# A new hand-written order for the first twelve blocks of an attention kernel, with P of blocks 0 to 3 transposed per token tile and 13 idle products instead of 22

## The chip, the core and the metric

The kernel runs on one core of one Trainium2 chip. The metric is the device time of one launch in microseconds (us). Three runs of the kernel before gave 808.72 us as their median (808.2 to 810.61). A difference under about 0.3% (2.4 us) cannot be told from no change.

## What is computed

The input `x` has 2048 tokens of 640 values and is layer-normalised to `xn`. Branch A is attention of 32 heads with 192 values per head, over the last 512 keys of a cache; branch B gives two selected tokens an extra feed-forward term and serves as a gate.

```
xn = layernorm(A_x)
q  = (xn @ wq) in 32 heads of 192
p  = softmax(q @ k_window^T * 192**-0.5)        # 512 keys
s  = concat(p @ v_window) @ wo
r  = xn @ w_r;  idx = the two tokens with the largest r
b  = xn, with sigmoid(r) * ffn(xn) added at idx
out = x + s * silu(b)
```

## The kernel before, in words

**Tiles and blocks.** The 32 heads are 8 groups of 4 heads, and a group is two pairs. The tokens are four stretches `t5` of 512, each of four token tiles of 128. A *step* is one group, one stretch and one pair of heads (`steps`); a *block* is half a step, that is two token tiles (a = 0, 1) of one pair of heads. There are 64 steps and 128 blocks, and blocks 0 and 1 belong to step 0, blocks 2 and 3 to step 1, and so on.

**The work of block b.** Q is the product of `xnT` with `wq` for a step, in three column parts c (`q_whole` in the head, L309, evicted to `qT` by ScalarE at L315 or VectorE at L313; from block 12 on, and for steps 5 to 7 in the head, in two phases `qa` and `qb` by `q_phase`, L340, evicted at L350 and L352). `S.b.a` is the scores of token tile a against the pair's keys (`scores`, L367), into one of two PSUM buffers `ps_s`. `M.b.a` is the negative row maximum on VectorE (L372). `E.b.a` is two exponentials on ScalarE (L377), one for each head, into `p_ring`; they also free the scores' buffer. P is then transposed by a DMA transpose on SyncE's queue into `pT_ring`: once for both token tiles after `E.b.1` (L383), or, for blocks listed in `SPLIT`, once after each `E.b.a` (L381). `P.b` is the product of pT with V (`o_item`, L406), whose result is scaled by the reciprocal of the row sums (L413) into `o_sb`: with "va" one head on VectorE (L417) and the other on ScalarE (L420), with "vv" both on VectorE, with "av" the two changed about. A DMA transpose makes `oT` (L423). `W.k` is the product of oT with `wo` (`w_item`, L447), added into `s_acc` by VectorE (L468) or, with "a", ScalarE (L466).

**The order.** The schedule is written by hand (`manual_schedule`): each engine runs its instructions in the order in which the Python code emits them. Blocks 0 to 11 (`HEAD = 12`) follow the list of tokens in `FIRST`, each passed to `first(token)`. From block 12 on all blocks follow the same list `BLOCK`, in which P lags by two blocks and W by six, and the last two follow `LAST`. The head also holds the layer norm: loads of x (`x.t5.part` and the loads ahead of the list), statistics (`bn`, `st` on VectorE, `sa` on ScalarE for three tiles of stretch 3), the reciprocal deviation (`dev`, `nw`), the normalisation of a token tile (`app`, `ap` on VectorE "v", ScalarE "a" or GpSimd "g"), and its transposition to `xnT` by TensorE and a copy (`turn`, L282 and L283), or for stretch 3 by one DMA transpose (`xT`, L515). `kturn` transposes the first pair's keys on TensorE (L276, copies at L277); for other pairs GpSimd reorders the keys (`ko`, L121) and a DMA transposes them (`kT`, L125). `v`, `k`, `wq`, `wo` are loads of their tensors on SyncE's queue; `wd` copies half of wo on GpSimd (L151). `exp` loads ScalarE's table for the exponential (L543). `B.b` emits the loads and other items that are due at block b.

**Queues.** All loads and DMA transposes of the list stand in SyncE's queue, in the order of their tokens; a transpose that waits for its data holds up what is behind it. Each DMA also waits for the DMA that last used its semaphore, and there are eight of these.

**Idle products.** Ahead of all this TensorE runs 22 products of a tile of zeros with itself (L163), whose result nobody reads, while the first loads and statistics are under way.

The block list that every block from 12 on follows, and the rule for the transposes of P:

```
    BLOCK = "A S0 M0 W m E0 B S1 M1 P E1 l".split()
...
        if b in SPLIT:
            nc.sync.dma_start_transpose(out=pT_ring[:, b % RP, a], ...
        elif a == 1 and b < NB - 1:
            nc.sync.dma_start_transpose(out=pT_ring[:, b % RP].rearrange(...
```

Of the kernel before, what the change touches and what calls it, by code (L numbers as in the profile page):

```python
# [21 lines left out]
def kernel(ctx, tc, A_x, A_k_cache, A_v_cache, A_wq, A_wo, B_x, B_w_r, B_w_gate, B_w_up, B_w_down, out):  # L22
    nc = tc.nc
    P = 128
    _, S, D = A_x.shape
# [3 lines left out]
    W = min(4096, max(256, Sk // 4))  # L29
# [44 lines left out]
    def f_tile(shape, dtype, name, kind="q"):  # L74
        return banks[kind].tile(shape, dtype, name=name, tag="f")
# [83 lines left out]
    idle = late.enter_context(tc.tile_pool(name="idle", bufs=1)).tile([P, W], BF16, name="idle")  # L159
    nc.vector.memset(idle, 0.0)  # L160
    warm_ps = f_tile([P, W], FP32, "warm_ps")
    for _ in range(22):
        nc.tensor.matmul(warm_ps, lhsT=idle[:, 0:P], rhs=idle, start=True, stop=True)  # L163

    ident_f = const.tile([P, P], FP32, name="ident_f")
# [121 lines left out]
    NS = len(steps)  # L287
    NB = 2 * NS
    HEAD = 12
    SPLIT = (NB - 4, NB - 3, NB - 2)  # L290
    qT_of = {}
    fin_x = {}
    fin_pool = {}
# [81 lines left out]
    def exps(b, a):  # L375
        for hh in range(2):
            nc.scalar.activation(out=p_ring[:, b % 2, a, :, hh, :].rearrange("p (x j) e -> p x j e", x=2),  # L377
                                 in_=s_of[b, a][:, hh, :].rearrange("p (j e x) -> p x j e", j=NJ, x=2),
                                 func=ACT.Exp, bias=nm_of[b, a][:, hh:hh + 1], scale=1.0)
        if b in SPLIT:  # L380
            nc.sync.dma_start_transpose(out=pT_ring[:, b % RP, a], in_=p_ring[:, b % 2, a].rearrange("p k h e -> p (k h e)"))  # L381
# [220 lines left out]

    def group_loads(g, b0, k0, k1, o0, t0, o1, t1, q0, q1, v0, v1, o):
# [20 lines left out]
    M = {}  # L624
# [232 lines left out]
    for fb, km in enumerate((41, 49, 57)):  # L857
# [4 lines left out]
        mul, turn = m_ffn(fb)  # L862
# [130 lines left out]
```

## Time and profile before

| | us |
|---|---|
| median of three runs | 808.72 |
| the profiled execution | 807.77 |
| its span, first to last instruction | 806.0 |
| TensorE busy | 783.0 (97%) |
| VectorE busy | 591.0 (73%) |
| ScalarE busy | 529.3 (66%) |
| GpSimd busy | 310.1 (38%) |

The profile is of one execution. Times in its views are microseconds from the start of the span. PE is TensorE's products, PEld its weight loads, DVE VectorE, ACT ScalarE, POOL GpSimd, and SPq the queue of DMA issues on SyncE; L367 is line 367 of the kernel before. Block 12, with which the fixed list begins, starts on TensorE at 90.61, so the part of the program that the change edits is the first 11% of the span. An instruction in a timeline lasts until its result is out, so that neighbours on one engine overlap a little; the chain of waits shows the distance at which they follow each other.

### The profile page before, as it was taken

The numbers are of one execution on the slowest core, as the hardware profiler recorded it, in microseconds if no ns is written. First come the engines' busy times: TensorE is split into PE (matmuls) and PEld (weight loads), VectorE is DVE, ScalarE is ACT, GpSimd is POOL, SyncE is SP. The second block draws the span as 40 slices with busy tenths as digits, with TensorE's granted clock in tenths as the row PEclk, the third lists the DMA queues.
The fourth block names the chain that finished last, engine by engine and source line by source line (L and its number), as shares of the span: only waits on it lengthen the run. The fifth ranks groups of instructions, "written<-read, shape, count | busy, mean of one in ns | idle before, by whom it ended". The sixth has DMA issues, their size and how long they took to land.

```text
span 806.0 us, 26621 instructions
## 1 busy us (share of the span) xinstructions
PE 783.0 (97%) x11354; PEld 579.1 (72%) x11354; DVE 591.0 (73%) x1086; ACT 529.3 (66%) x964; POOL 310.1 (38%) x244
## 2 busy tenths in 40 slices
PE   8799899999999999999999999999999999999997
PEld 4366577777777777777777777777777777777775
DVE  7686588778778667777666667777777777767775
ACT  5677566665666666666666667677776776666662
POOL 1312120011110100101011699959997412564865
PEclk9999999999999999999999999999999999999999
DMA  7998998798999999999998999989898899999992
GB/s 193 188 175 161 199 169 154 152 189 143 191 199 160 181 208 200 196 188 191 200 211 159 171 192 166 182 137 184 173 186 149 153 190 163 209 190 163 178 181 84
DMA packets 445111, 142.29 MB, mean 177 GB/s; under 512 B 412228, under 2 KB 444488, under 8 KB 444992
## 3 DMA queue, kind: packets, MB, share of 16 engines
q1 hardware_dynamic: 435216, 131.18, 93.1%
q10 hardware_dynamic: 8816, 6.88, 3.3%
q0 software_dynamic: 960, 2.52, 1.0%
q8 instruction: 89, 1.46, 0.8%
q14 instruction: 30, 0.25, 0.1%
HBM read 39.98 MB, written 2.62 MB: 53 GB/s over the span
## 4 chain that ended last, share of the span: by engine, by line
PE 85%; DVE 5%; DMA 4%; ACT 3%; issue 2%; POOL 0%; SPq 0%; ACTq 0%; DVEq 0%; POOLq 0%
PE w L447 24%; PE q_ps L340 21%; PE o_ps L406 18%; PE s L367 18%; DVE nm L372 2%; DMA pT<-pexp 2%; PE q_ps L309 2%; ACT o_sb L420 1%; ACT pexp L377 1%; PE warm_ps L163 1%; DMA xnT<-xn 1%; DMA oT<-o_sb 1%; DMA wo_g<-in_A_wo_dram 1%; DMA v_sb<-in_A_v_cache_dram 0%; ACT qT L315 0%
## 5 line engine op out<-in xcount | busy, mean ns | idle before, releaser
L372 DVE TENSOR_REDUCE nm<-s 128x2 f32<-128x1024 f32 x256 | 313.0, 1223 | 135.6 <-PE s L367 131.0
L377 ACT ACTIVATE pexp<-s,nm 128x512 bf16<-128x512 f32 x512 | 323.3, 688 | 90.3 <-DVE nm L372 53.9
L447 PE MATMUL w<-wo_g,oT 64*128 64x320 bf16 x3072 | 231.1, 296 | 4.8 <-ACT o_sb L420 4.5
L340 PE MATMUL q_ps<-xnT,wq_g 64*128 64x512 bf16 (+1 forms) x2340 | 232.4, 323 | 3.2 <-DMA xnT<-xn 1.5
L447 PEld LDWEIGHTS <-oT 64*128 64x128 bf16 x3072 | 171.8, 94 | 62.9 <-issue 7.5
L367 PE MATMUL s<-kT,qT 64*128 64x512 bf16 x1536 | 211.7, 376 | 5.0 <-ACT pexp L377 3.9
L406 PEld LDWEIGHTS <-pT 64*128 64x128 bf16 x4096 | 179.1, 94 | 27.9 <-issue 2.0
L406 PE MATMUL o_ps<-v_sb,pT 64*128 64x193 bf16 x4096 | 197.2, 243 | 0.0
L420 ACT ACTIVATE o_sb<-o_ps,rl 128x192 bf16<-128x192 f32 x256 | 93.6, 417 | 145.7 <-DVE rl L413 140.6
L340 PEld LDWEIGHTS <-wq_g 64*128 64x128 bf16 x2340 | 127.4, 99 | 48.3 <-issue 2.6
L151 POOL COPY wo_g<-wo_g 64x1920 bf16<-64x1920 bf16 x32 | 59.3, 1858 | 222.3 <-DMA wo_g<-in_A_wo_dram 202.1
L367 PEld LDWEIGHTS <-qT 64*128 64x128 bf16 x1536 | 85.4, 94 | 59.8 <-issue 6.4
L470 DVE TENSOR_TENSOR s_acc<-s_acc,w 128x320 f32<-128x320 f32 x192 | 85.0, 484 | 35.4 <-PE w L447 35.4
L352 ACT ACTIVATE qT<-q_ps 128x1024 bf16<-128x1024 f32 x114 | 92.4, 810 | 7.7 <-PE q_ps L340 2.8
L121 POOL COPY k_perm<-k_raw 128x768 bf16<-128x768 bf16 x30 | 25.1, 854 | 143.3 <-DMA k_raw<-in_A_k_cache_dram 111.9
L417 DVE TENSOR_TENSOR o_sb<-o_ps,rl 128x384 bf16<-128x384 f32 x128 | 71.4, 558 | 4.6 <-DVE rl L413 0.2
L831 POOL TENSOR_SCALAR yh<-y_bc,oh 128x640 bf16<-128x640 bf16 x32 | 61.7, 1929 | 3.3 <-DMA y_bc<-y_d 1.7
L832 POOL TENSOR_TENSOR xn<-xn,yh 128x640 bf16<-128x640 bf16 x32 | 44.6, 1395 | 2.7
L413 DVE RECIPROCAL rl<-o_ps 128x2 f32<-128x2 f32 x256 | 30.0, 159 | 14.4 <-PE o_ps L406 8.2
L894 POOL TENSOR_TENSOR s_acc<-s_acc,x_fin 128x640 f32<-128x640 f32 x16 | 22.4, 1397 | 31.3 <-DMA x_fin<-in_A_x_dram 30.8
L828 POOL TENSOR_SCALAR xn<-xn 128x640 bf16<-128x640 bf16 x16 | 29.4, 1838 | 0.8
L478 POOL TENSOR_TENSOR fin_o<-fin_t,s_acc 128x640 bf16<-128x640 f32 x12 | 18.5, 1540 | 17.7 <-DVE fin_t L473 11.1
(138 smaller groups left out, 262.4 us busy)
## 6 DMA issues: line engine op xcount, KB each, us to landing
wo_g<-in_A_wo_dram SPq DMA_DIRECT2D x32, 240.0 KB, 4.3
k_raw<-in_A_k_cache_dram SPq DMA_DIRECT2D x32, 192.0 KB, 3.6
v_sb<-in_A_v_cache_dram SPq DMA_DIRECT2D x32, 192.0 KB, 4.3
wq_g<-in_A_wq_dram SPq DMA_DIRECT2D x14, 288.0 KB, 4.1
wq_g<-in_A_wq_dram SPq DMA_DIRECT2D x14, 192.0 KB, 3.7
x_fin<-in_A_x_dram SPq DMA_DIRECT2D x16, 160.0 KB, 3.6
pT<-pexp SPq DMA_TRANSPOSE x130, 4.9
oT<-o_sb SPq DMA_TRANSPOSE x126, 3.4
```

What stands on the lines that cost most here:

```text
L151: nc.gpsimd.tensor_copy(out=grp[g][("wo", pr)][half(1), cs, :], in_=grp[g][("wo", pr)][half(0), cs, :])
L340: mm = nc.tensor.matmul(q_ps[k][:, 0:n] if type(q_ps) is list else q_ps[:, k, 0:n], lhsT=wq[half(r), dc, c:2 * Dh:3], rhs=xnT[half(r), tok ...
L352: nc.scalar.activation(out=out, in_=q_ps[:, :, 0:n], func=ACT.Copy, scale=scale)
L367: nc.tensor.matmul(s_of[b, a][:, r, :], lhsT=qT_of[i][half(r), c, u * P:(u + 1) * P], rhs=grp[g][("kT", pr)][half(r), :, c, :], start=(c = ...
L372: rm = nc.vector.tensor_reduce(out=nm_of[b, a], in_=s_of[b, a], axis=AX.X, op=ALU.max, negate=True)
L377: nc.scalar.activation(out=p_ring[:, b % 2, a, :, hh, :].rearrange("p (x j) e -> p x j e", x=2), in_=s_of[b, a][:, hh, :].rearrange("p (j ...
L406: nc.tensor.matmul(o_of[b][r][:, a, 0:Dh + 1], lhsT=pT_ring[half(r), b % RP, a, k, :], rhs=v_ring[half(r), (g * PAIRS + pr) % RV, k, 0:Dh ...
L417: nc.vector.tensor_tensor(out=o_sb, in0=src, in1=rl[:, r].unsqueeze(2).unsqueeze(3).to_broadcast([P, 2, 3, HK]), op=ALU.mult)
L420: nc.scalar.activation(out=o_sb[:, a], in_=src[:, a], func=ACT.Copy, scale=rl[:, r, a:a + 1])
L447: nc.tensor.matmul(w_ps[r][:, 0:HD], lhsT=oT_ring[half(r), bs[pr] % RT, c, :], rhs=grp[g][("wo", pr)][half(r), c, cs], start=(pr == 0 and ...
L470: nc.vector.tensor_tensor(out=acc, in0=acc, in1=src, op=ALU.add)
L831: nc.gpsimd.tensor_scalar(out=yh, in0=M["y_bc"][:, j, :], scalar1=M["oh"][:, n, j:j + 1], scalar2=None, op0=ALU.mult)
```

## The change

`FIRST` is written anew: the same tokens, with few exceptions, in another order. Besides the order:

- 13 idle products instead of 22;
- `SPLIT` holds blocks 0 to 3 too, so the P of each of their token tiles is transposed by a DMA of its own, as soon as that tile's exponentials are done;
- some evictions, normalisations and scalings go to another engine: `q.0.0.0` and `q.0.2.1` from VectorE to ScalarE, all of `q.2`, `q.4.1` and `q.6.2` from ScalarE to VectorE, the copies of `turn.3` and `turn.4` from ScalarE to VectorE and those of `turn.2` and `turn.6` the other way, `ap.4` to ScalarE, `ap.5`, `ap.7`, `ap.9`, `ap.14` from VectorE to GpSimd, `ap.6` and `ap.15` from GpSimd to VectorE, `ap.13` from ScalarE to GpSimd, `W.0` from ScalarE to VectorE, `W.3` and `W.5` the other way, and P.0, P.7 and P.8 are scaled by VectorE alone;
- `wq.1`, `x.1.1`, `v.1` and `x.2` are issued further ahead of the other DMAs, and the statistics of stretch 1 follow the first row maxima.

Everything from block 12 on is unchanged in the source.

```diff
-    for _ in range(22):
+    for _ in range(13):
...
-    SPLIT = (NB - 4, NB - 3, NB - 2)
+    SPLIT = (0, 1, 2, 3, NB - 4, NB - 3, NB - 2)
...
     FIRST = """
-    bn.1.0 x.1.0 bn.0.0 bn.0.1 v.0 v.1 dev.0 bn.1.1 dev.1 app.0 turn.0.a app.1 bn.3.0 turn.1.a bn.2.0 bn.2.1 dev.2 bn.3.1 kturn.av k.1.0 k.1.1 ko.1 wq.1 x.1.1 dev.3 exp st.1.0 q.0.0.0.v app.2 q.0.1.0.a kT.1 app.3 q.0.2.0.a turn.2.v turn.3.a st.1.1
-    S.0.0 S.0.1 M.0.0 q.0.0.1.a M.0.1 q.0.1.1.a q.0.2.1.v E.0.0 q.1.0.a E.0.1 v.2 v.3
-    S.1.0 st.1.2 M.1.0 st.1.3 S.1.1 M.1.1 q.1.1.a E.1.0 st.1.4 q.1.2.a E.1.1 st.1.5 st.1.6 st.1.7 x.2 wo.0 wo.1 wo.2
-    S.2.0 M.2.0 nw.1.0 nw.1.1 S.2.1 M.2.1 nw.1.2 nw.1.3 E.2.0 nw.1.4 nw.1.5 nw.1.6 ap.6.g P.0.va E.2.1 ap.4.v ap.7.v ap.5.v wo.3 wd.0 wd.1
-    S.3.0 M.3.0 turn.4.a turn.7.v S.3.1 M.3.1 turn.5.a turn.6.v E.3.0 q.2.0.a q.2.1.a P.1.va E.3.1 x.3 wd.2 wd.3 st.2.0 st.2.1 q.2.2.a st.2.2
-    S.4.0 M.4.0 q.3.0.a S.4.1 E.4.0 M.4.1 st.2.3 q.3.1.a P.2.va E.4.1 st.2.4 st.2.5 st.2.6 st.2.7
-    S.5.0 nw.2.0 M.5.0 q.3.2.a S.5.1 nw.2.1 nw.2.2 E.5.0 M.5.1 nw.2.3 nw.2.4 nw.2.5 nw.2.6 P.3.va E.5.1 ap.10.g ap.8.v sa.3.0.0
-    S.6.0 M.6.0 E.6.0 W.0.a S.6.1 M.6.1 ap.9.v ap.11.v P.4.va E.6.1 sa.3.0.1 sa.3.2.0 st.3.6 B.6
-    S.7.0 M.7.0 turn.8.v turn.11.v W.1.v turn.9.a turn.10.v S.7.1 M.7.1 E.7.0 P.5.va q.4.0.a q.4.1.a q.4.2.a E.7.1 B.7 sa.3.1.0 sa.3.2.1 st.3.7 sa.3.1.1
-    qa.5.0.1 S.8.0 B.8 nw.3.0 M.8.0 nw.3.1 nw.3.2 W.2.v qb.5.0.1 nw.3.3 S.8.1 M.8.1 E.8.0 nw.3.4 nw.3.5 nw.3.6 P.6.va E.8.1 ap.13.a ap.15.g ap.14.v ap.12.v xT.3
-    qa.5.2 S.9.0 M.9.0 B.9 W.3.v E.9.0 qb.5.2 S.9.1 M.9.1 P.7.va E.9.1
-    S.10.0 M.10.0 W.4.v E.10.0 S.10.1 M.10.1 P.8.va B.10 E.10.1
-    qa.6.0.1 S.11.0 M.11.0 W.5.v E.11.0 qb.6.0.1 S.11.1 M.11.1 P.9.va q.6.2.a E.11.1 B.11
+    v.0 bn.1.0 x.1.0 bn.0.0 bn.0.1 dev.0 bn.1.1 app.0 dev.1 x.1.1 app.1 turn.0.a wq.1 bn.3.0 bn.3.1 turn.1.a bn.2.0 v.1 k.1.0 bn.2.1 st.1.0 dev.3 k.1.1 kturn.av q.0.0.0.a dev.2 app.2 q.0.1.0.a
+    q.0.2.0.a app.3
+    S.0.0 turn.2.a x.2 v.2 ko.1 exp kT.1 turn.3.v S.0.1 q.0.1.1.a M.0.0 E.0.0 M.0.1 st.1.1 q.0.0.1.a st.1.2 q.0.2.1.a E.0.1 q.1.0.a wo.0
+    S.1.0 st.1.3 st.1.4 q.1.1.a v.3 M.1.0 st.1.5 wo.1 S.1.1 M.1.1 E.1.0 q.1.2.a E.1.1 st.1.6
+    S.2.0 st.1.7 nw.1.0 S.2.1 nw.1.1 nw.1.2 M.2.0 nw.1.3 M.2.1 wo.2 nw.1.4 E.2.0 nw.1.5 nw.1.6 E.2.1 P.0.vv ap.7.g
+    S.3.0 ap.6.v turn.7.v ap.5.g ap.4.a M.3.0 turn.4.v wd.0 st.2.0 wd.1 turn.6.a turn.5.a E.3.0 S.3.1 P.1.av wo.3 x.3 M.3.1 q.2.0.v wd.2 E.3.1 q.2.1.v st.2.1 q.2.2.v st.2.2
+    S.4.0 st.2.3 st.2.4 S.4.1 M.4.0 P.2.va E.4.0 q.3.1.a M.4.1 E.4.1 st.2.5 st.2.6 q.3.2.a st.2.7 wd.3
+    S.5.0 nw.2.0 nw.2.1 nw.2.2 M.5.0 q.3.0.a S.5.1 nw.2.3 nw.2.4 M.5.1 nw.2.5 E.5.0 W.0.v
+    S.6.0 M.6.0 nw.2.6 E.5.1 ap.10.g ap.11.v sa.3.0.0 sa.3.2.0 B.6 ap.9.g P.3.va E.6.0 S.6.1 M.6.1 P.4.va ap.8.v W.1.v E.6.1
+    S.7.0 turn.10.v turn.11.v turn.9.a turn.8.v S.7.1 st.3.6 sa.3.0.1 sa.3.1.0 M.7.0 B.7 E.7.0 q.4.1.v st.3.7 q.4.2.a M.7.1 q.4.0.a
+    qa.5.0.1 sa.3.2.1
+    S.8.0 E.7.1 M.8.0 B.8 W.2.v sa.3.1.1 nw.3.0 nw.3.1 qb.5.0.1 nw.3.2 nw.3.3 nw.3.4 nw.3.5 nw.3.6 P.5.va S.8.1 ap.13.g E.8.0 M.8.1 P.6.av E.8.1 ap.15.v ap.14.g
+    qa.5.2
+    S.9.0 S.9.1 M.9.0 ap.12.v E.9.0 qb.5.2 xT.3 M.9.1
+    S.10.0 B.9 M.10.0 E.9.1 W.3.a S.10.1 P.7.vv E.10.0 P.8.vv M.10.1 W.4.v
+    qa.6.0.1
+    S.11.0 B.10 E.10.1 M.11.0 W.5.a qb.6.0.1 P.9.va B.11 q.6.2.v S.11.1 M.11.1 E.11.0 E.11.1
     """.split()
```

## The prediction

> **What bounds the kernel now.** I read three views in this order: the busy time of each engine by stretch, TensorE's waits in the part that is edited, and TensorE's timeline there. By stretch (columns: from:to, length, then busy us of PE, PEld, DVE, ACT and POOL, granted clock, DMA share, GB/s):
>
> ```profile
> 9.00:90.61 81.61, 70.95 (x834) 43.72 (x831) 59.33 (x126) 58.96 (x121) 18.02 (x26) 1.00 0.91 176
> 90.61:180.00 89.39, 87.11 (x1276) 65.51 (x1277) 70.97 (x128) 55.88 (x101) 14.10 (x17) 1.00 0.97 169
> 180.00:404.00 224.00, 221.62 (x3305) 166.10 (x3303) 163.70 (x321) 144.59 (x261) 24.92 (x22) 1.00 1.05 187
> ```
>
> From block 12 (90.61) on TensorE is the bound: it idles 2.28 us of 89.39 and 2.38 of 224. Nothing there hangs on a fixed time, so a head that ends earlier moves all that follows. In the head TensorE idles 81.61 - 70.95 = 10.66 us, and before 9.00 it runs idle products. TensorE's largest waits up to 90.7 (total, times, longest):
>
> ```profile
> PE s L367 <- ACT pexp L377: 3.9, 5, 1.0
> PE q_ps L340 <- DMA xnT<-xn: 1.5, 1, 1.5
> PE q_ps L309 <- DVE xnT L283: 1.4, 1, 1.4
> PE tp L282 <- DVE xn L193: 1.3, 1, 1.3
> ```
>
> So it waits mostly for latency: scores for a free buffer, Q for a normalised tile. VectorE and ScalarE are busy 59 of 81.6 us, so it is their order, not their load, that makes TensorE wait. That is what a new order can win. The landmarks on TensorE:
>
> ```profile
> 1.19 7.71 PE L163 MATMUL warm_ps<-idle 128*128 128x512 bf16 x22 [1.19 <-DVE idle L160]
> 13.27 1.47 PE L367 MATMUL s<-kT,qT 64*128 64x512 bf16 x12
> 23.26 0.88 PE L367 MATMUL s<-kT,qT 64*128 64x512 bf16 x6 [0.76 <-ACT pexp L377]
> 46.41 0.82 PE L367 MATMUL s<-kT,qT 64*128 64x512 bf16 x6 [0.34 <-ACT pexp L377]
> 82.12 1.26 PE L340 MATMUL q_ps<-xnT,wq_g 64*128 64x512 bf16 x10 [1.48 <-DMA xnT<-xn]
> 90.61 1.26 PE L340 MATMUL q_ps<-xnT,wq_g 64*128 64x512 bf16 x10 [0.69 <-ACT qT L315]
> ```
>
> These are the idle products, S.0.0 with S.0.1, S.2.0, S.5.1, the first phase of qa.6.0.1 and the start of block 12.
>
> **The idle products.** Their weight loads show the pace:
>
> ```profile
> 6.28 0.15 PEld L163 LDWEIGHTS <-idle 128*128 128x128 bf16 x1 [0.28 <-issue]
> 6.71 1.69 PEld L163 LDWEIGHTS <-idle 128*128 128x128 bf16 x8 [0.28 <-issue]
> ```
>
> ```profile
> PEclk9999999999999999999999999999999999999999
> ```
>
> Up to 6.71 one product takes 0.43 us, after that 1.69 / 8 = 0.21: TensorE's pace doubles near 7, after 5.5 us at half. The page's clock row shows nothing of it, so only the pace tells. Thirteen at 0.43 end at 1.19 + 5.55 = 6.74, not 8.9. The first work behind them needs the first normalised tile, whose statistics come in the same order on VectorE as before:
>
> ```profile
> 5.99 0.45 DVE L264 TENSOR_SCALAR xn<-x_in,mv,rstd 128x640 bf16<-128x640 bf16 x1
> 18.43 1.23 DVE L372 TENSOR_REDUCE nm<-s 128x2 f32<-128x1024 f32 x1 [1.08 <-PE s L367]
> 36.88 0.56 DVE L417 TENSOR_TENSOR o_sb<-o_ps,rl 128x384 bf16<-128x384 f32 x1
> ```
>
> Ready at 6.44, it waited 2.4 us for the products; now 0.3. So 2.1 us is won at that point, if the pace is not lost. [...] What a late switch costs I bound from the rows by themselves: a second spell at half pace as long as the first, 5.5 us from 6.74 on, loses at most half of it, so 0 to 2.8. I take 0.5, near the low end, because the work that follows starts at once and the copies between leave room.
>
> **The walk through the new order.** I walked the new list by hand, each engine in its order, with these durations. TensorE's distances, from the chain of waits:
>
> ```profile
> 112.03 1.64 PE w L447 x24
> 113.67 0.55 PE q_ps L340 x10
> 114.22 0.65 PE s L367 x6
> 114.86 1.35 PE o_ps L406 x32
> 116.21 1.08 PE q_ps L340 x10
> ```
>
> ScalarE and GpSimd:
>
> ```profile
> 9.21 1.29 ACT L283 COPY xnT<-tp 128x640 bf16<-128x640 bf16 x2 [2.95 <-PE tp L282]
> 10.58 0.80 ACT L277 COPY kT<-tp_k 128x768 bf16<-128x768 bf16 x1
> 11.59 1.28 ACT L543 ACT_TABLE_LOAD   x1
> 21.95 1.26 ACT L377 ACTIVATE pexp<-s,nm 128x512 bf16<-128x512 f32 x2
> 35.15 0.60 ACT L315 ACTIVATE qT<-q_ps 128x512 bf16<-128x512 f32 x1 [0.48 <-PE q_ps L309]
> ```
> ```profile
> 12.55 1.72 POOL L121 COPY k_perm<-k_raw 128x768 bf16<-128x768 bf16 x2 [10.76 <-DMA k_raw<-in_A_k_cache_dram]
> ```
>
> DMA transposes (issue in ns, min/median/max; landing after the issue; the first two rows are the head's whole transposes of P, the next two the tail's, mostly of one token tile):
>
> ```profile
> L383 SPq DMA_TRANSPOSE pT<-pexp x11: 1697/1992/5461, 19.4 to 88.9; - x11
> DMA to landing us min/median/max: 4.3/4.5/9.1
> ```
> ```profile
> L381 SPq DMA_TRANSPOSE pT<-pexp x6: 1232/1323/2166, 770.9 to 782.7; - x6
> DMA to landing us min/median/max: 3.1/4.8/5.2
> ```
> ```profile
> kT<-k_perm SPq DMA_TRANSPOSE x2, 3.9
> xnT<-xn SPq DMA_TRANSPOSE x1, 6.9
> ```
>
> *To S.0.0.* Transposes of tiles 0 and 1 and of the keys (about 0.3, 0.3, 0.7 at full pace) run from 6.74 to 8.3; ScalarE copies the two tiles by 8.4; three Q products of 256 columns (0.55 each, 1.65) end at 10.2; ScalarE's last eviction ends at 10.75. The statistics `st.1.0` now stand ahead of VectorE's copy of the keys and wait for x of stretch 1, so that copy ends near 10.5, just in time. S.0.0 starts at 10.8, not 13.27: 2.5 us.
>
> *To S.2.0.* S.0.1 follows only after tiles 2 and 3 (12.05), since their normalisation stands behind. The maxima end at 13.65 and 14.8; the table load (1.28, now behind the copy of tile 2) ends at 13.7; with three evictions between, E.0.0 ends at 15.2 and E.0.1 at 16.95. S.1.0 starts at 15.85, S.1.1 at 17.6, the evictions of q.1 end at 20.0, and S.2.0 starts at 20.05, not 23.26: 3.2 us. The keys of the pair must be there: loads land near 12.2, GpSimd's copies (1.72) end at 13.9, the transpose lands near 18.4. `x.2` is issued ahead of it, its 640 KB, as slow as the row below, spend that margin at worst.
>
> ```profile
> x_in<-in_A_x_dram SPq DMA_DIRECT2D x2, 640.0 KB, 6.0
> SPq L383 <- ACT pexp L377: 19.4, 8, 3.7
> ```
>
> *To S.4.0 and S.5.1.* The split counts here. P.0 starts at 21.95. E.0.1 ends at 16.95, the second half is issued at 17.0 and lands 4.8 later, at 21.8. SyncE issues 2 x 1.32 instead of 1.99 for a block, 2.6 us more over four; its queue waited 19.4 us for exponentials at L383 alone (the row above, SyncE's waits up to 100), which hides that, and if the queue fills it costs up to 2.6. Tiles 4 to 7 are normalised on three engines while P.0 and S.3.0 run, so the two waits of 1.3 and 1.4 for them shrink to one of 0.9. The evictions of q.2 go to VectorE, which ends them at 32.65 while ScalarE does E.3.1 (31.55). S.4.0 is over at 33.1 and S.5.1 starts at 39.25, not 46.41: 7.2 us.
>
> *To block 12.* W.0 is late next: its oT of block 2 is issued at 36.3 and I let W.0 start at 40.5, a wait of 0.6. From S.6.0 to P.6 the walk finds TensorE with work all the time, though ScalarE has the statistics of stretch 3 among its exponentials. Then S.9.1 waits 1.2 for E.8.1 and S.10.0 0.8 for an eviction. `xT.3` goes out at 65.5 behind pT of block 8, lands at 72.4, and qa.6.0.1 starts at 73.0, so the wait of 1.5 for it goes. The rest is work as before, less the last 0.69: block 12 at 80.6.
>
> **The sum.** The walk gives 90.61 - 80.6 = 10.0. Three terms take from it. First, stalls that it does not show. From 9.00 to block 12 TensorE was busy 70.95, while the walked distances of the same work add up to about 67; so some 4 us of small bank and hand-off stalls lie inside the rows, and the walk holds about 1. That leaves 0 to 3.3; I take 2. Second, the pace, 0 to 2.8; 0.5. Third, the DMA. The head moved 81.61 us x 176 GB/s = 14.4 MB; at the 187 GB/s of the stretch to 404 this takes 76.8 us, and block 12 would start at 85.8. That is 0 to 5.2 on the walk; I take 0.5, because the 187 was measured where TensorE, not the DMA, set the pace. Block 12 starts at 83.6, 7.0 us earlier. The profiled execution took 807.77 (span 806.0), so it becomes 800.8; the median of the runs shown is 0.95 above that execution, and I forecast on its scale **801.7**.
>
> **Rivals.** (1) *The pace stays at half through the first scores.* For it: 13 products end at 6.74, and the doubling came near 7. Against: the work behind is dense. Price 2.8 instead of 0.5: 804.0. [...] (2) *The lead is given back.* For it: DMA share 0.97 and 1.05 after block 12, so a queue that is behind at block 12 has little room to catch up, and exponentials that wait for a buffer of P hold all. Against: TensorE idles about 1% there. It costs most of the 7.0, say 6.5: 808.2. (3) *Slower, by landings.* The same 14.4 MB in 74.6 us is 193 GB/s, above every stretch of the table. If landings double, as the 9.1 against 4.5 shows can be, the second half of P.0 lands at 26.1 and TensorE waits 4.2, and xnT takes 13.8, lands at 79.3 and costs 6.3. That is 10.5 on the walk, with the 2.0 of stalls and the 0.5 of the clock 93.6 for block 12: 3.0 us later, 811.7. It decides from landings of about 1.75 times the median on; below that the head still wins. Against: the loads that are moved ahead fill stretches in which the DMA engines stood still:
>
> ```profile
> 10.00:11.00 1.00, 0.57 (x8) 0.44 (x6) 0.84 (x2) 1.00 (x3) 0.00 (x0) 1.00 0.04 7
> 18.00:19.00 1.00, 0.39 (x4) 0.09 (x1) 0.57 (x1) 1.00 (x3) 0.00 (x0) 1.00 0.00 0
> ```
>
> **How the numbers follow.** My forecast, with block 12 between 80 and 86.5, gets 0.60; rival 1 0.13, rival 2 0.14, rival 3 0.13. Faster by over 0.3% (2.4 us, about what a measurement tells from no change; below 806.3) is the forecast and rival 1, 0.73; within, rival 2, 0.14; slower, rival 3, 0.13. The range: the whole walk gives 798.7, and 1.2 less for terms that I may have too high, 797.5; above, it takes in rival 1 and rival 2, to 808.5. Rival 3 and the far ends lie outside.
>
> **What would show it.** Idle products over by 6.8, S.0.0 at 10.5 to 12.5, S.2.0 at 20 to 22, P.0 without a long DMA wait, S.5.1 at 39 to 42, qa.6.0.1 without a wait for xnT, and block 12 at 80 to 86.5 with the time behind it as before (806.0 - 90.61 = 715.4). I am wrong if TensorE's weight loads still follow each other at the half pace beyond 10.5, if P.0 or xnT lands late, or if those 715.4 us grow.

## The result, and the profile after

| | before | after | ratio |
|---|---|---|---|
| median, us | 808.46 | 803.0 | 0.993 [0.9902, 0.9958] |
| lowest to highest of 6 runs | 806.06 to 810.63 | 799.61 to 806.9 | |
| profiled execution, span | 807.77, 806.0 | 806.4, 804.6 | |

The change gains 5.5 us; 7.0 were forecast, and the range held the time. The profiled execution of after is one of its longest, so I use two more profiles of the same kernel (called the second and the third, from the runs `e1_after_again` and `e12_after_third`), and a second one of before.

TensorE's timeline of after, the same landmarks as in the prediction: idle products, the transposes of the keys, S.0.0, S.2.0, P.1, S.5.1, W.0, the first phase of qa.6.0.1, P.9, block 12 and P.10.

```profile
1.18 5.73 PE L163 MATMUL warm_ps<-idle 128*128 128x512 bf16 x13 [1.18 <-DVE idle L160]
...
8.66 0.83 PE L276 MATMUL tp_k<-ident,k_raw 128*128 128x128 bf16 x12 [1.04 <-DMA k_raw<-in_A_k_cache_dram]
...
12.07 0.82 PE L367 MATMUL s<-kT,qT 64*128 64x512 bf16 x6 [0.94 <-DVE kT L277]
...
21.31 0.92 PE L367 MATMUL s<-kT,qT 64*128 64x512 bf16 x6 [0.16 <-DVE nm L372]
...
29.85 1.74 PE L406 MATMUL o_ps<-v_sb,pT 64*128 64x193 bf16 x32 [0.74 <-DMA pT<-pexp]
...
42.57 0.82 PE L367 MATMUL s<-kT,qT 64*128 64x512 bf16 x6
44.96 0.99 PE L447 MATMUL w<-wo_g,oT 64*128 64x320 bf16 x12 [0.75 <-DMA oT<-o_sb]
...
77.03 1.37 PE L340 MATMUL q_ps<-xnT,wq_g 64*128 64x512 bf16 x10
...
82.50 1.52 PE L406 MATMUL o_ps<-v_sb,pT 64*128 64x193 bf16 x32 [0.75 <-DMA pT<-pexp]
86.00 1.26 PE L340 MATMUL q_ps<-xnT,wq_g 64*128 64x512 bf16 x10
...
93.13 1.52 PE L406 MATMUL o_ps<-v_sb,pT 64*128 64x193 bf16 x32 [1.86 <-DMA pT<-pexp]
```

It shows that the first thing that is late is no longer the products but the keys (a wait of 1.04 for `k_raw`), that the wait of 1.48 ahead of qa.6.0.1 is gone, and that block 12 starts 4.61 us earlier (90.61 - 86.00). By stretch (columns as in the prediction), the head and the 94 us behind it:

```profile
8.66:86.00 77.34, 70.26 (x825) 43.22 (x825) 60.14 (x127) 54.96 (x111) 19.80 (x27) 1.00 0.97 184
86.00:180.00 94.00, 90.66 (x1336) 69.00 (x1337) 74.18 (x136) 58.77 (x106) 15.00 (x18) 1.00 1.01 169
```

In the head TensorE idles 7.08 us, not 10.66. Behind block 12 it idles 3.34 of 94, where before it idled 2.28 of 89.

The executions differ, so here are the landmarks of all profiles of the two kernels (starts on TensorE; "behind" is the span less the start of block 12), with the forecast:

| | S.0.0 | S.2.0 | S.5.1 | block 12 | behind |
|---|---|---|---|---|---|
| before | 13.27 | 23.26 | 46.41 | 90.61 | 715.4 |
| before, second | 12.80 | 22.80 | 45.95 | 90.19 | 717.4 |
| forecast (S rows: the walk) | 10.8 | 20.05 | 39.25 | 83.6 | 715.4 |
| after | 12.07 | 21.31 | 42.57 | 86.00 | 718.6 |
| after, second | 10.81 | 20.09 | 40.53 | 82.02 | 718.6 |
| after, third | 10.90 | 20.19 | 40.69 | 82.98 | 721.5 |

On the mean of the profiles block 12 starts 6.7 us earlier (90.4 against 83.7), and the time behind it is 3.2 us longer (719.6 against 716.4). The head did what the forecast says; a part of it is given back. (6.7 less 3.2 is 3.5, not the 5.5 of the medians: two of the three profiles of after are among the longest executions of their runs.) To see where, I followed the lead, the start of each W in the first profile of before less its start in the other profile. W.125 is the first of the last three, which run as one; the last row is the kernel of the section "Both mended" below.

| | W.0 | W.6 | W.7 | W.8 | W.20 | W.67 | W.80 | W.125 |
|---|---|---|---|---|---|---|---|---|
| before, second | 0.5 | 0.4 | 0.4 | 1.4 | 0.1 | -0.5 | -0.7 | -1.6 |
| after | 7.0 | 4.6 | 2.4 | 3.5 | 3.7 | 5.4 | 2.9 | 1.6 |
| after, second | 9.0 | 8.6 | 6.3 | 7.4 | 6.9 | 9.1 | 7.2 | 5.6 |
| after, third | 8.9 | 7.6 | 5.5 | 6.6 | 6.5 | 4.4 | 3.7 | 1.8 |
| both mended | 8.8 | 7.7 | 8.5 | 9.6 | 10.7 | 13.2 | 11.2 | 10.2 |

All three of after lose about 2.2 us between W.6 and W.7, near 93 us. About 1.05 of it comes back at W.8, where the kernel before itself waits 0.87; by W.20 they have lost 0.9 to 1.7, and the second profile of before 0.3. The larger loss lies behind W.67: 2.6 to 3.8 us up to W.125, against 1.1 in the second profile of before. The first and the second lose 2 to 2.5 of it between W.67 and W.80 (460 to 540 us), where the third loses 0.7 behind an earlier loss.

**At W.7.** Three views of after around that place, SyncE's queue, GpSimd and VectorE:

```profile
83.39 1.34 SPq L125 DMA_TRANSPOSE kT<-k_perm  x1
84.78 1.02 SPq L136 DMA_DIRECT2D v_sb<-in_A_v_cache_dram  x1
85.91 3.99 SPq L383 DMA_TRANSPOSE pT<-pexp  x1
```
```profile
87.35 1.59 POOL L121 COPY k_perm<-k_raw 128x768 bf16<-128x768 bf16 x2 [16.90 <-DMA kT<-k_perm]
88.89 0.76 POOL L636 DMA_DIRECT2D wr_bc<-in_B_w_r_dram  x1
```
```profile
92.83 0.82 DVE L652 SCALAR_TENSOR_TENSOR junk<-xn,wr_bc 128x640 bf16<-128x640 bf16 x1 [2.31 <-DMA wr_bc<-in_B_w_r_dram]
```

The same place before, on SyncE, GpSimd, VectorE and TensorE (P.10):

```profile
88.94 3.73 SPq L383 DMA_TRANSPOSE pT<-pexp  x1
```
```profile
91.33 0.76 POOL L632 DMA_DIRECT2D wr_bc<-in_B_w_r_dram  x1
```
```profile
95.30 0.82 DVE L648 SCALAR_TENSOR_TENSOR junk<-xn,wr_bc 128x640 bf16<-128x640 bf16 x1 [0.19 <-DMA wr_bc<-in_B_w_r_dram]
```
```profile
95.69 1.53 PE L406 MATMUL o_ps<-v_sb,pT 64*128 64x193 bf16 x32
```

The chain: SyncE transposes the keys of the next pair at 83.39; GpSimd's copy of the keys after them waits for that (`k_perm` has one buffer); the load of the router's weights `w_r` stands behind the copy in GpSimd's order (88.89); VectorE's first router product (`junk`) waits 2.31 for the load, and in VectorE's order it stands ahead of the maxima M.12.1, of P.10's scaling and so of W.7, whose products go into the PSUM buffers that this scaling frees. `m_open`, which issues this load, is put at block 11 outside of `FIRST`, the list that I walked. Beside it P.10 waits 1.86 for its pT, whose transpose was issued at 85.91 behind the transfers of `B.9` and `B.10`, the items due at blocks 9 and 10, which the list emits ahead of E.9.1 and E.10.1. The list before did so too, and P.10 did not wait: the queue's order is the old one, and TensorE comes to it earlier.

### The profile page after: what moved, and what is told of

It is laid out like the page before. It is cut to its first block, busy times and chain, and to the rows that moved or that the text cites. A ratio compares the mean times of both kernels' runs of the same rounds, so it can differ in the third digit from the quotient of the medians.

```text
span 804.6 us, 26603 instructions
## 1 busy us (share of the span) xinstructions
PE 781.8 (97%) x11345; PEld 578.4 (72%) x11345; DVE 592.1 (74%) x1087; ACT 527.7 (66%) x957; POOL 314.3 (39%) x247
## 4 chain that ended last, share of the span: by engine, by line
PE 83%; DMA 8%; DVE 5%; ACT 2%; issue 1%; DVEq 0%; ACTq 0%
PE w L447 24%; PE q_ps L340 21%; PE o_ps L406 18%; PE s L367 18%; DMA pT<-pexp 6%; DVE nm L372 2%; DMA x_in<-in_A_x_dram 1%; PE q_ps L309 1%; ACT pexp L377 1%; DVE xn L845 1%; ACT o_sb L420 1%; DMA oT<-o_sb 1%; DVE s_acc L470 0%; DVE o_sb L417 0%; ACT qT L352 0%
## 5 line engine op out<-in xcount | busy, mean ns | idle before, releaser
L420 ACT ACTIVATE o_sb<-o_ps,rl 128x192 bf16<-128x192 f32 x250 | 91.6, 418 | 144.2 <-DVE rl L413 138.6
L151 POOL COPY wo_g<-wo_g 64x1920 bf16<-64x1920 bf16 x32 | 60.0, 1876 | 225.9 <-DMA wo_g<-in_A_wo_dram 200.8
L417 DVE TENSOR_TENSOR o_sb<-o_ps,rl 128x384 bf16<-128x384 f32 x131 | 73.1, 558 | 4.7 <-DVE rl L413 0.2
L836 POOL TENSOR_TENSOR xn<-xn,yh 128x640 bf16<-128x640 bf16 x32 | 44.7, 1397 | 2.7
L832 POOL TENSOR_SCALAR xn<-xn 128x640 bf16<-128x640 bf16 x16 | 30.4, 1901 | 0.8
L478 POOL TENSOR_TENSOR fin_o<-fin_t,s_acc 128x640 bf16<-128x640 f32 x12 | 18.5, 1541 | 17.5 <-DVE fin_t L473 11.2
```

The costliest lines, as they stand in the source:

```text
L151: nc.gpsimd.tensor_copy(out=grp[g][("wo", pr)][half(1), cs, :], in_=grp[g][("wo", pr)][half(0), cs, :])
L417: nc.vector.tensor_tensor(out=o_sb, in0=src, in1=rl[:, r].unsqueeze(2).unsqueeze(3).to_broadcast([P, 2, 3, HK]), op=ALU.mult)
L420: nc.scalar.activation(out=o_sb[:, a], in_=src[:, a], func=ACT.Copy, scale=rl[:, r, a:a + 1])
```

## The experiments

What was to be told apart. **Theory:** the gain is the order of the head, which takes out waits for latency; products and split are worth little by themselves; what is lost again goes at W.7, to the two transfers that come late there, w_r and pT. **Rivals:** the products are the gain; the split costs or gains; late keys cost the head; the longer rest is only that the first profile of before had a short one. The order of the list, the changes of engine and the loads issued earlier were not taken apart from each other; "order" means the three together. The runs were measured in three groups (`e1` to `e4`, `e5` to `e8`, `e9` to `e12`), each beside runs of the kernel before, whose medians were 807.78, 809.07 and 808.72. Each ratio is against those.

### The kernel after once more, unaltered

> The changed kernel once more, unaltered, as the base of comparison for the other runs. Theory A (the order wins the time in the head): block 12 starts within 1 us of the 86.0 of the first profile, the ratio to before is 0.990 to 0.996, and the 3.2 us by which the time behind block 12 was longer in the first profile than in the profile of before vary from execution to execution by 1 to 3 us. Theory B (the head wins 4.6 us, but the order makes the rest longer): the time behind block 12 is again 718 to 719 us, not 715.

Measured (`e1_after_again`): 804.22 (9 runs), ratio 0.9948 [0.9925, 0.9972]. The profile's block 12 starts 4 us earlier than in the first profile, which I had not expected: the keys had landed in time (transposes at 7.32 with no wait, S.0.0 at 10.81 as walked). The rest is 718.6 us again, as theory B says, and the wait for pT at P.10 is there too:

```profile
89.23 1.52 PE L406 MATMUL o_ps<-v_sb,pT 64*128 64x193 bf16 x32 [1.95 <-DMA pT<-pexp]
```

It follows that when the keys land decides about 1.3 us at S.0.0, and that the head of a single profile is no measure finer than some 4 us.

### 22 idle products in the kernel after

```diff
-    for _ in range(13):
+    for _ in range(22):
```

> The changed kernel with 22 idle products. Theory A: the products end at 8.9, tiles 0 and 1 are transposed 2.2 us later, but the keys of the first pair landed only at 8.6 and the copy of their second half waited for x until 11.06, so S.0.0 starts at 12.6 to 13.2, not 12.07; block 12 0.5 to 1.2 us later than in the changed kernel; ratio to before 0.992 to 0.998. Rival (the 9 products were most of the gain): S.0.0 at 14 or later, block 12 at 88 or later, ratio 0.997 to 1.0.

Measured (`e2_after_22`): 806.62 (12 runs), 0.9974 [0.9951, 0.9997]. The head hardly suffers: S.0.0 at 12.27, a little earlier than expected, block 12 at 83.06, between the profiles of after. But behind it VectorE waits 4.54 for w_r and W.7 2.56 for what VectorE holds up. VectorE, then TensorE, then TensorE's stretches of 1 us:

```profile
92.12 0.82 DVE L652 SCALAR_TENSOR_TENSOR junk<-xn,wr_bc 128x640 bf16<-128x640 bf16 x1 [4.54 <-DMA wr_bc<-in_B_w_r_dram]
```
```profile
94.99 2.32 PE L447 MATMUL w<-wo_g,oT 64*128 64x320 bf16 x20 [2.56 <-ACT o_sb L420]
```
```profile
95.00:96.00 1.00, 1.00 (x13) 0.74 (x13) 0.96 (x1) 1.00 (x3) 0.91 (x1) 0.79 0.27 56
96.00:97.00 1.00, 1.00 (x10) 0.73 (x8) 0.00 (x0) 1.00 (x3) 0.00 (x0) 0.50 2.62 145
```

The granted clock (the column after POOL) falls to 0.50 until 99, after the pause and while TensorE already works again. So the products are not the gain in the head, and the place at W.7 has two prices, the wait and the clock. But the whole kernel is not as fast as after: its median is 2.4 us above that of `e1_after_again`, measured beside it (a 95% interval of the difference of the two medians, by resampling the runs, is 0.8 to 4.7). With 22 products less than half of the gain is left. Why nine products more at the start make w_r later at W.7, I can't say.

### The split taken back

```diff
-    SPLIT = (0, 1, 2, 3, NB - 4, NB - 3, NB - 2)
+    SPLIT = (NB - 4, NB - 3, NB - 2)
```

> The changed kernel with the P of blocks 0 to 3 transposed whole. Theory A (the split is worth little): pT of block 0 goes out after E.0.1 and the keys' transpose, at 19.8, and lands at 24.2 to 24.5, so P.0 waits 0.5 to 0.9; P.1 waits about as it did; block 12 0 to 1.2 us later; ratio 0.991 to 0.997. Rival (the split carries the new order): P.0 and P.1 wait 2 us each, block 12 at 88 or later, ratio 0.996 or more.

Measured (`e3_after_whole`): 803.15 (12 runs), 0.993 [0.9907, 0.9954]: as after. P.0 waits for nothing, P.1 waits 1.32 where it waited 0.74, block 12 starts at 84.66.

```profile
23.63 1.52 PE L406 MATMUL o_ps<-v_sb,pT 64*128 64x193 bf16 x32
...
30.14 1.10 PE L406 MATMUL o_ps<-v_sb,pT 64*128 64x193 bf16 x22 [1.32 <-DMA pT<-pexp]
```

The split is worth nothing that can be measured.

### 13 idle products in the kernel before

```diff
-    for _ in range(22):
+    for _ in range(13):
```

> The kernel before with 13 idle products, nothing else changed. Theory A: its keys land earlier than in the changed kernel, since fewer loads run beside them, so the first Q product starts 1.5 to 2.1 us earlier; a part of it is lost at waits behind; block 12 at 88.5 to 90, ratio 0.997 to 1.0. Rival (the 9 products were most of the gain): block 12 at 87.5 or earlier, ratio 0.993 to 0.997. If the pace of TensorE stays at half beyond 10 us, block 12 is as late as before or later.

Measured (`e4_before_13`): 810.12 (12 runs; 805.9 to 815.2), 1.0021 [0.9995, 1.0046], which is no change; theory A had the first Q right, but not block 12 and not the ratio. TensorE's weight loads, then TensorE:

```profile
3.72 0.15 PEld L163 LDWEIGHTS <-idle 128*128 128x128 bf16 x1 [0.28 <-issue]
4.15 1.00 PEld L163 LDWEIGHTS <-idle 128*128 128x128 bf16 x5 [0.28 <-issue]
...
6.64 0.28 PEld L282 LDWEIGHTS <-xn 128*128 128x128 bf16 x5 [1.50 <-DVE xn L264]
```
```profile
81.48 1.26 PE L340 MATMUL q_ps<-xnT,wq_g 64*128 64x512 bf16 x10 [1.94 <-DMA xnT<-xn]
...
91.65 1.26 PE L340 MATMUL q_ps<-xnT,wq_g 64*128 64x512 bf16 x10 [0.69 <-ACT qT L315]
```

The first Q starts 2.07 us earlier, S.5.1 still 1.1 earlier, but qa.6.0.1 then waits 1.94 instead of 1.48 for xnT and is only 0.6 earlier. Behind that wait the granted clock falls, from 82.7 to 86.1, and block 12 is later than before:

```profile
83.00:84.00 1.00, 1.00 (x10) 0.33 (x8) 0.00 (x0) 0.00 (x0) 0.00 (x0) 0.50 1.16 227
```

In this order the earlier start runs into the next wait and gains nothing. In the new order, where that wait is gone, the nine products do make a difference, though it shows at W.7 and not in the head (`e2_after_22`).

### The keys loaded first

```diff
-    v.0 bn.1.0 x.1.0 ... dev.1 x.1.1 app.1 turn.0.a wq.1 bn.3.0 ... bn.2.0 v.1 k.1.0 bn.2.1 st.1.0 dev.3 k.1.1 kturn.av q.0.0.0.a ...
+    bn.1.0 x.1.0 ... dev.1 app.1 turn.0.a bn.3.0 ... bn.2.0 v.0 bn.2.1 st.1.0 dev.3 kturn.av k.1.0 k.1.1 wq.1 x.1.1 v.1 q.0.0.0.a ...
```

> The changed kernel with the loads v.0, v.1, wq.1 and the second half of x of stretch 1 issued behind the second pair's keys, as the kernel before has most of them. Theory C (the loads that the change moves ahead run beside the first pair's keys and make them land late, by 0 to 1.3 us from execution to execution): the keys' transposes start at 7.4 to 7.7 without a wait, S.0.0 at 10.3 to 11, block 12 at 81 to 83 in every execution; ratio to before 0.990 to 0.995, a narrower spread than the 799.6 to 806.9 of the changed kernel. Rival: the keys' landing is chance that no order of loads alters; S.0.0 at 10.8 to 12.1 as before, or wq.1 now lands late and q.1 waits.

Measured (`e5_keys_first`): 806.05 (12 runs), 0.9959 [0.9937, 0.9982]. The keys need no wait and S.0.0 starts at 10.24, but the ratio and block 12 (85.39) miss what was expected. The loads only moved: kT of pair 1 stands behind them in SyncE's queue and its issue takes 7.35 us, so S.2.0 waits 3.47. SyncE, then TensorE:

```profile
12.61 7.35 SPq L125 DMA_TRANSPOSE kT<-k_perm  x1
```
```profile
10.24 0.93 PE L367 MATMUL s<-kT,qT 64*128 64x512 bf16 x6
...
23.70 1.04 PE L367 MATMUL s<-kT,qT 64*128 64x512 bf16 x8 [3.47 <-DMA kT<-k_perm]
```

Loading the keys first took their wait away and put another in its place; it gained nothing.

### P's transposes ahead of the loads of B.9 and B.10

```diff
-    S.10.0 B.9 M.10.0 E.9.1 W.3.a ...
+    S.10.0 M.10.0 E.9.1 B.9 W.3.a ...
...
-    S.11.0 B.10 E.10.1 M.11.0 W.5.a ...
+    S.11.0 E.10.1 B.10 M.11.0 W.5.a ...
```

> The changed kernel with the loads of blocks 9 and 10 (B.9, B.10) behind E.9.1 and E.10.1 in SyncE's queue, so that the transposes of P of blocks 9 and 10 go ahead of them. Theory D (P.10's wait of 1.9 to 2.1 us and P.9's of up to 0.75 come from loads ahead of pT in SyncE's queue): both waits are gone, block 12 as in the changed kernel or 0.7 earlier, W.7's lead is not lost, and the pause that let the granted clock fall to half for 3.4 us in two of the profiles does not arise: 2 to 3 us in time, ratio 0.989 to 0.994. Rival (the DMA engines are full there, the order in the queue does not matter): P.10 waits 1 us or more all the same, or the keys of step 8 come late and something else waits as long.

Measured (`e6_p_first`): 808.48 (12 runs), 0.9992 [0.9971, 1.0014]: the whole gain is gone. The waits at P.9 and P.10 did go, as theory D says, but as in the second half of the rival something else waits as long: kT lands later, and with it w_r. VectorE, TensorE, and TensorE's stretches:

```profile
93.95 0.82 DVE L652 SCALAR_TENSOR_TENSOR junk<-xn,wr_bc 128x640 bf16<-128x640 bf16 x1 [6.55 <-DMA wr_bc<-in_B_w_r_dram]
```
```profile
87.98 1.51 PE L406 MATMUL o_ps<-v_sb,pT 64*128 64x193 bf16 x32
...
96.81 1.52 PE L447 MATMUL w<-wo_g,oT 64*128 64x320 bf16 x10 [6.13 <-ACT o_sb L420]
```
```profile
95.00:96.00 1.00, 0.00 (x0) 0.00 (x0) 1.00 (x3) 0.00 (x0) 0.00 (x0) 0.55 0.00 0
...
101.00:102.00 1.00, 1.00 (x10) 0.46 (x6) 0.83 (x3) 0.60 (x1) 0.00 (x0) 0.53 0.63 137
```

That shows both halves of the theory at the head of The experiments: the order of SyncE's queue makes the waits at P, and the chain by w_r holds W.7, here for 6.13 us with a clock of half until 101.9 behind it.

### Both of these edits

> Both edits, keys first and P first. Theories C and D together: block 12 at 81 to 83, no wait at P.9 and P.10, median 799 to 802, ratio 0.988 to 0.992, so ahead of both kernels. Rival: 803 to 804, as the changed kernel.

Measured (`e7_both`): 813.02 (12 runs), 1.004 [1.0015, 1.0064], slower than before. Both faults are there, S.2.0 at 22.89 after a wait of 2.64 and the lead of 6.1 at W.6 down to 0.5 at W.7; the clock is at half from 23.2 to 26.6 and from 94.9 to 101.7. The faults add, neither hides the other.

### The kernel before once more

> The kernel before once more, for a second profile. Theory E (the time behind block 12 varies from execution to execution by waits between 460 and 650 us, where GpSimd is busy nearly all the time, and the first profile of before had few of them): behind block 12 716 to 719 us, not 715.4, with block 12 at 89.5 to 91.5. Theory B (the new head makes the rest longer): again 715 to 716.

Measured (`e8_before_again`): 809.38 (one run), block 12 at 90.19, 717.4 us behind it, as theory E says, though not at the place that it names: W.67 to W.95 take 166.4 us against 166.0. So 2 us of the difference in the time behind block 12 between the first profiles is the execution; against 718.6, 718.6 and 721.5 some 1 to 4 us are left.

### w_r loaded two blocks earlier

```diff
-    bg[11].append(m_open)
+    bg[9].append(m_open)
```

> The changed kernel with the load of w_r for the router (and the small set-up beside it on GpSimd) emitted at block 9, not at block 11, so that on GpSimd it stands ahead of the reordering of keys that waits for the transpose of the pair before. Theory F (the time that the new head loses at W.7 is a chain: transpose of the keys, reordering on GpSimd, load of w_r, VectorE's first router product, the scaling of P.10, W.7): VectorE no longer waits 2.3 to 6.6 us for w_r. P.10 still waits 1.5 to 2 us for its pT, so W.7's lead falls by 1 to 2 us rather than 2.2 to 3.5; fewer pauses long enough for the clock to fall; ratio 0.990 to 0.995. Rival (P.10's pT is all of it): no difference from the changed kernel.

Measured (`e9_wr_early`): 802.8 (6 runs), 0.992 [0.9897, 0.9943]. VectorE's wait is gone, and P.10 still waits 1.34 for pT, so W.7 still loses 1.7 us of the lead. The load of w_r alone is worth about 0.5 of the 2.2 there:

```profile
87.69 0.82 DVE L652 SCALAR_TENSOR_TENSOR junk<-xn,wr_bc 128x640 bf16<-128x640 bf16 x1
```

### Both mended

The edits of `e6_p_first` and `e9_wr_early` together:

> P of blocks 9 and 10 ahead of the loads in SyncE's queue, and w_r loaded early. Theory F: each of the two waits at P.10 hid the other, so that the edit of the queue alone only made the other longer (6.1 us at W.7 and a clock at half for 6 us); with both edits neither is there, W.6's lead of 5 to 8.6 us is kept at W.8, the clock stays at 1.0 to the end; ratio 0.987 to 0.992, median 1 to 3 us below the changed kernel of the same call. Rival (the transposes of keys and the loads that now stand behind P stall something else): a new wait of over 1 us between 84 and 110 us.

Measured (`e10_p_first_wr_early`): 801.46 (6 runs; 797.81 to 802.87), 0.9912 [0.9891, 0.9932]. From 70 to 110 us, after and this kernel:

```profile
70.00:110.00 40.00, 36.58 (x519) 26.24 (x517) 25.31 (x46) 21.34 (x41) 5.67 (x12) 1.00 1.07 182
```
```profile
70.00:110.00 40.00, 39.92 (x580) 29.02 (x577) 28.86 (x54) 23.51 (x44) 5.63 (x4) 1.00 1.10 196
```

TensorE is busy 39.92 of 40 us, where it was 36.58. The lead is 7.7 at W.6, 8.5 at W.7 and 10.7 at W.20, since waits are gone that the kernel before has there too. This shows that the two transfers together took the lead at W.7. The time behind block 12 (82.85) is 713.2, less than in any profile of before, but the profile is of the fastest of the six executions, and from W.67 to W.125 it too loses 3.0 us. The median is 1.7 us below that of after, measured beside it (803.15, "The kernel after a third time"), with intervals that overlap.

### Both mended, without the split

The edits of `e10_p_first_wr_early` and of `e3_after_whole`:

> The same, with the P of blocks 0 to 3 transposed whole again. Theory A: the split is worth under 1 us, since whole transposes landed within 1.3 us of P.1's need and cost SyncE 2.6 us less; within 1.5 us of the run with the split. Rival: 2 us or more slower.

Measured (`e11_p_wr_whole`): 800.7 (6 runs; 799.65 to 801.24), 0.9898 [0.988, 0.9917]; block 12 at 83.04, 715.3 behind it. Its median is the lowest of all, 2.5 us below that of after, measured beside it: the intervals of the ratios overlap, but each of its six runs is faster than each of the six of after (801.98 to 806.78). Again the split brings nothing.

### The kernel after a third time

> The changed kernel, unaltered, on the chip of this call, as the base for the three others. Block 12 between 82 and 86, a drop of W.7's lead by 2 to 3.5 us, ratio 0.992 to 0.996.

Measured (`e12_after_third`): 803.15 (6 runs), 0.9933 [0.9908, 0.9958]; block 12 at 82.98, and the loss of 2.1 at W.7 as in the other two.

## Why the prediction was right or wrong

**Right, and for its reason: the head.** The new order is what made the head shorter. Where the keys land in time, the walk holds to 0.1 us at S.0.0 and S.2.0 (10.81 and 20.09 for 10.8 and 20.05) and to 1.3 at S.5.1 (40.53 for 39.25). Block 12, forecast at 83.6, started at 82.0, 83.0 and 86.0. The wait of W.0, forecast at 0.6, was 0.75 in the first profile, 0.64 in the third and none in the second; that for xnT went.

**The step on the keys was optimistic.** "Transposes of tiles 0 and 1 and of the keys ... run from 6.74 to 8.3" takes the keys as landed. In the first profile they waited 1.04 for them, and S.0.0 came 1.27 late. In the second and the third it held, with the same loads issued early, so that these loads make the keys late is argued, not shown. (One of the loads named under The change did not move ahead: SyncE issues `v.1` at 7.07, and before right behind `v.0` at 3.83.)

**The products.** The 2.1 us "won at that point" are real (2.07 in the kernel before), but alone worth nothing (`e4_before_13`). In the new order 22 products cost the head nothing that shows, and yet the whole kernel 2.4 us (`e2_after_22`), so the gain in time belongs to the order with the 13 products, not to the order alone. The walk did not see that: it priced the products by the start of the first work.

**The pace.** I took 0.5 of 0 to 2.8; it is near 0. That dense work brings the doubling, on which I counted, no run shows. After 13 products the pace doubled at the latest in the transposes behind them. In the first profile of after all 13 run at the half pace, and the weight loads of the transposes are 0.10 us apart up to the third and 0.056 from there, 10 of them in 0.83 us; in the third profile the doubling comes behind the sixth gap:

```profile
5.85 0.15 PEld L163 LDWEIGHTS <-idle 128*128 128x128 bf16 x1 [0.28 <-issue]
...
6.61 0.83 PEld L282 LDWEIGHTS <-xn 128*128 128x128 bf16 x10 [0.61 <-DVE xn L264]
```

Rival 1 is out. **The split**, on which the walk counted for P.0, is worth nothing that shows: without it P.0 waits for nothing and P.1 1.3 us (`e3_after_whole`, `e11_p_wr_whole`), and the time is the same. **The stalls**, 2 of 0 to 3.3: that banks or hand-offs make up the 4 us between the 70.95 busy and the about 67 walked, no run shows; block 12 came 1.4, 2.4 and 5.4 us behind the walk's 80.6, and how much of that is such stalls is not shown either. **The DMA**, 0.5 of 0 to 5.2, showed as waits of 0.74 at P.1, 0.75 at W.0 and 0.75 at P.9 in the first profile, beside the 1.04 for the keys; 0.64 in the third, none in the second. Rival 3 is out: TensorE's longest wait for a landing in that head is the 1.04 for the keys.

**Wrong: what lies behind block 12.** The step that failed is "Nothing there hangs on a fixed time, so a head that ends earlier moves all that follows", and with it the 715.4 us taken as they were. Two things were not seen. First, transfers that P.10 and W.7 need hang on the chain of loads and transposes on SyncE and GpSimd, which the new list brings forward less than TensorE and VectorE. In the first profile of after, TensorE is ready for P.10 at 93.13 - 1.86 = 91.27 instead of 95.69, 4.4 us earlier, but its pT is issued at 85.91 instead of 88.94, 3.0 earlier. The load of w_r is issued at 88.89 instead of 91.33, 2.4 us earlier; VectorE is ready for its product at 92.83 - 2.31 = 90.52 instead of 95.30 - 0.19 = 95.11, 4.6 us earlier. TensorE itself waits there for pT, and w_r is late right behind it: mending one alone leaves 1.7 us of the loss (`e9_wr_early`) or makes it 5.5 (`e6_p_first`), mending both leaves none (`e10_p_first_wr_early`). I counted the moved loads in the head, not the queue at block 12, though rival 2 names "a queue that is behind at block 12" as its reason. It is rival 2 in small: 2.2 us at W.7, of which 0.9 to 1.7 are still missing at W.20. Second, 715.4 was itself the low one of two profiles of before, and after loses 2.6 to 3.8 us behind W.67, more than at W.7. Why is the next point.

**What stays open.** Between W.67 and W.95 (464.88 to 630.91 before, 459.44 to 628.74 after) the same work takes 3.3 us longer, in `e10_p_first_wr_early` 1.9. The stretch before and after, and VectorE's group of it that changes:

```profile
464.88:630.91 166.03, 165.43 (x2466) 125.62 (x2463) 126.64 (x209) 117.03 (x210) 139.89 (x86) 1.00 0.98 172
```
```profile
L841 DVE SCALAR_TENSOR_TENSOR xn<-tz,xn 128x640 bf16<-128x640 f32 x13 | 12.5, 961 | 0.0
```
```profile
459.44:628.74 169.30, 166.38 (x2466) 125.52 (x2464) 129.43 (x209) 117.65 (x210) 146.29 (x90) 1.00 0.97 171
```
```profile
L845 DVE SCALAR_TENSOR_TENSOR xn<-tz,xn 128x640 bf16<-128x640 f32 x13 | 16.4, 1259 | 0.0
```

VectorE takes 2.8 us more for the same 209 instructions, and GpSimd has 4 instructions more in the stretch. It lies in that one group of 13, whose own time grows from 12.5 to 16.4 us: of its products that start while GpSimd's L832 (L836 after) runs, 54 of 55 end 0.68 or 0.69 us behind it (see the end of this text). Over the fourteen profiles VectorE's time and the length go together: 126.6 to 127.6 us of VectorE and lengths of 166.0 to 166.6 in the three with the old order; 127.8 and 127.9 with 166.5 and 166.8 in `e5_keys_first` and the third of after; 128.6 to 129.9 with 167.3 to 169.3 in the nine others. GpSimd starts its long block there later against TensorE: 5.4 to 6.8 us ahead of W.67 with the old order, 1.4 to 3.2 ahead with the new. The load of the vector `y_bc` before it lands 4.1 to 4.9 us after its issue with the old order and 6.9 to 8.2 with the new. GpSimd in before, then in after:

```profile
453.88 0.59 POOL L824 DMA_DIRECT2D y_bc<-y_d  x1 [1.65 <-DMA y_d<-y_sb]
...
458.12 1.89 POOL L831 TENSOR_SCALAR yh<-y_bc,oh 128x640 bf16<-128x640 bf16 x1 [1.74 <-DMA y_bc<-y_d]
```
```profile
450.03 0.60 POOL L828 DMA_DIRECT2D y_bc<-y_d  x1 [3.20 <-DMA y_d<-y_sb]
...
458.09 1.88 POOL L835 TENSOR_SCALAR yh<-y_bc,oh 128x640 bf16<-128x640 bf16 x1 [5.54 <-DMA y_bc<-y_d]
```

That these products end so soon behind GpSimd's instruction is measured; that GpSimd's later start makes more of them do so, and that this makes the stretch longer, is argued only: no run moved that load or that block alone, and why the load lands later is open.

## What to carry to other kernels

When the head of a tuned kernel gets faster, walk on past its last line to the first items that another engine starts on its own order or due time (here a load of weights behind a copy behind a transpose): they move less than the head does, and the lead shrinks there. Two late transfers at one place have to be mended together; moving one ahead of the other alone cost this kernel its whole gain. What an earlier start of the first work is worth hangs on the waits behind it: nothing in the order before, some 2.4 us in the new one.

## What the runs showed of the hardware

**The granted clock fell to 0.50 in mid-run at some pauses.** It went to 0.50 for 3.4 us after TensorE had waited 1.94 us (`e4_before_13`), 2.07 (`e3_after_whole`), 2.56 (`e2_after_22`) and 2.64 (`e7_both`), and for 6.8 us around waits of 6.13 (`e6_p_first`) and 6.23 (`e7_both`); in the first four the fall came 0.3 to 1.2 us after the work had gone on, in the last two during the pause. It did not fall behind waits of 1.86, 1.95 and 1.77 (P.10 in the three profiles of after), nor of 3.47 in `e5_keys_first`. So in these runs it is not the length of the pause alone; what else it is, no run shows.

**The pace doubled at different times.** The idle products' weight loads go from 0.43 to 0.21 us apart at 3.72 (second of before), 4.15 (`e4_before_13`), 5.74 (second of after) and 6.71 us (before and `e2_after_22`). In the first of after all 13, up to 5.85, run at 0.43. What sets the time, no run shows.

**The issue of a DMA transpose of keys took 1.34 to 7.35 us.** The issue of one DMA transpose of keys on SyncE took 1.34 us at 83.39 in after, and 7.35 and 5.97 us behind loads in `e5_keys_first` and `e7_both`. That the loads ahead of it make it long is not shown.

**75 of 77 products of VectorE that started during an instruction of GpSimd ended 0.68 or 0.69 us behind it.** VectorE's router product (L648 before, L652 after) takes 0.81 to 0.83 us while GpSimd is idle, 153 times in the fourteen profiles. Of the 22 that start while GpSimd copies wo (L151), 21 end 0.68 us after the copy does, and take up to 2.43; the 35 during which this copy starts take 0.81 or 0.82. It is the same for the group L841 (before; L845 after) beside GpSimd's L832 (L836): of 55 that start while it runs, 54 end 0.68 or 0.69 us after it. So beside these copies the time grew where GpSimd's instruction started first, and not where VectorE's did. Behind such a product W.8 waits in the kernel before; VectorE, GpSimd and TensorE:

```profile
101.64 2.28 DVE L648 SCALAR_TENSOR_TENSOR junk<-xn,wr_bc 128x640 bf16<-128x640 bf16 x1
```
```profile
101.46 1.78 POOL L151 COPY wo_g<-wo_g 64x1920 bf16<-64x1920 bf16 x1 [7.97 <-DMA wo_g<-in_A_wo_dram]
```
```profile
105.96 1.81 PE L447 MATMUL w<-wo_g,oT 64*128 64x320 bf16 x24 [0.87 <-ACT o_sb L420]
```
